# Transposes in 64-row halves, gathered in large groups, and inverse rows moved to other PSUM tiles, in a fused convolution and gated-MLP training step

## The chip, the cores and the metric

The kernel runs on one core of a Trainium2 chip, as one launch. The metric is the device time of that launch in microseconds. A core has a matrix engine (TensorE, here PE, with weight loads listed apart as PEld), a vector engine (VectorE, DVE), a scalar engine (ScalarE, ACT), GpSimd (POOL) and SyncE (SP). SP, ACT and POOL each have a queue from which they issue DMA transfers. SBUF is the working memory with 128 partitions; PSUM, in eight banks of 2 KB a partition, is where PE writes.

## What is computed

The reference is a forward pass and its gradient with respect to nine inputs:

```python
xn = layernorm(A_q)                                  # 2048 rows, 1024 columns
kv = shifted(A_k, A_shift_k) * A_v                   # four taps
y  = irfft(rfft(kv, 4096) * rfft(A_ssm_k, 4096))[:2048] + kv * A_ssm_D
s  = xn * y
h  = (xn @ w_gate) * (xn @ w_up)                     # 3584 columns
g  = silu(h @ w_down)
out = A_q + s * g
# then: gradients of all nine inputs for grad_out
```

All inputs and outputs are bfloat16. The long convolution runs down the rows, one for each of the 1024 columns.

## The kernel before

A Tile scheduler places the instructions of each engine; a few are pinned to their program order. PE does its work strictly in that order. The stages are:

*Layer norm and first gate blocks (to about 60 us).* `layer_norm` normalizes row blocks of 128. PE turns each 128x128 piece by a transpose (a matmul with the identity `ident`) into a PSUM tile `tr` of the pool `ps_st`, ACT copies it to `XNT`. The last eight blocks are put into `turn_rows` and turned later by `turn_late` (L617, L618), which `gu_unit` calls.

*The forward stage (60 to about 555 us).* `gu_unit` (L656 to L693) computes the gate and up products for four row blocks of one slab of 256 columns: for each block eight matmuls of 512 columns (1.7 us) into `psg`, an ACT copy to `gut`, then `flush(5)`, which calls what was put off five blocks earlier with `defer`. `multiply` makes the product `hN` on DVE, and stores it. `turn` transposes `hN` in eight 128x128 pieces (L689) into the one PSUM tile of the pool `ps_tr` (one bank), ACT copies them to `hT` (L691), and `store` writes `hT` to `HTd` on SP's queue. There are 14 slabs of 16 row blocks.

Between the blocks stands the convolution, `conv_forward`, a generator: `pump` runs it forward after each block as far as a planned share of its DVE work (`F_TOTAL`, less 0.95 times the PE work that `pe_us` counts). For each of eight column groups `ds` of 128 it does: `h_rows` (16 transposes of filter rows, L752 and L754, in two groups of eight through `ps_tr`, each with an ACT copy to `hx`); forward transforms of filter and data (`fwd4_half` or `fwd8_half`: PE matmuls into `psF` of the pool `ps_cv`, two tiles of two banks, ACT copies to `SP`, then sums on DVE); `product` and the inverse (`inv_dft` or `inv8`) on DVE into `HX`; and one column group later `tail`: the inverse rows, matmuls of `HX` with the table `TI` (`inv8_rows` L446, `inv_rows` L457) into `psY` of the pool `ps_y` (one bank), two rows at a time in four steps, each with an ACT copy to `yf` (L773). The table `TI` is made by `turn_tables` (L193) in four groups, also through `psY`. During the forward stage PSUM is full: `ps_y` 1, `ps_tr` 1, `ps_gu` 2, `ps_cv` 4 banks.

*Down projection and gates (about 508 to 710 us).* `bm_mm` (L994) multiplies `HTd`'s rows with `w_down`, 28 pairs of 512-column matmuls a row block, into `psbm`. The last column group's four tail steps stand behind pairs 52, 55, 58 and 61 of the late row blocks, by the tuple `at`. `gate` does each row block on DVE: `so`, `gg`, `dbm`, `dy` and others.

*The rest (710 to 1917 us)*: gradients, dense matmuls (L1441, L1458, L1541, L1603) with the backward convolution beside them.

`st` and `cld` issue on POOL's queue (L66), `ld` on SP's (L61), `sta` on ACT's (L72); `tt` is a DVE operation (L213), `stt` another (L284).

Of the kernel before, what the change touches and what calls it, by code (L numbers as in the profile page):

```python
# [19 lines left out]
def build_kernel(  # L20
# [11 lines left out]
    nc = tc.nc  # L32
# [153 lines left out]
    def turn_tables(psp):  # L186

        for j in range(2):
            for rq in range(2):
                ps = psp.tile([P, 4, 2, P], BF16, name="psY")  # L190
                for i in range(4):
                    for k in range(2):
                        nc.tensor.transpose(ps[:, i, k, :], T4[j][:, 4 * rq + i, k, :], ident[:])  # L193
                nc.scalar.copy(out=TI[:, j, 4 * rq:4 * rq + 4], in_=ps[:])
                yield

# [251 lines left out]

    def inv_rows(G, psp, rp):

        ps = psp.tile([P, 2, 256], F32, name="psY")
        for i in range(2):
            r = 2 * rp + i
            n = 0
            for j in range(2):
                for k in range(2):
                    nc.tensor.matmul(ps[:, i, :], TI[:, j, r, k, :], gseg(G, r, j, k),  # L457
                                     start=(n == 0), stop=(n == 3))
                    n += 1
        return ps  # L460

# [60 lines left out]
    fg = pool("fg", 2, side="right")  # L522
    ps_y = pool("ps_y", 1, space=PSUM)
    ps_tr = pool("ps_tr", 1, space=PSUM)
    ps_gu = pool("ps_gu", 2, space=PSUM)
    ps_st = pool("ps_st", 4, space=PSUM)

    busy = ps_st.tile([P, 4, P], F32, name="tr")

# [33 lines left out]
    turn_rows = []  # L563

    def layer_norm(b0, n, x4):
        def small(name, dt=F32):
# [21 lines left out]
        for i in range(n):  # L588
            b = b0 + i
            q, qi = divmod(b, 4)  # L590
            last = V.tensor_scalar(x4[:, i, :], x4[:, i, :], mv[:, i, 0:1], RSTD[:, b:b + 1], op0=SUB, op1=MUL)
            if b < 2:
                for hh in range(2):
                    ps = ps_st.tile([P, 4, P], BF16, name="tr")
                    for dc in range(4):
                        d0 = (4 * hh + dc) * P
                        tr_ln[0] = nc.tensor.transpose(ps[:, dc, :], x4[:, i, d0:d0 + P], ident[:])
                    act_copy[0] = nc.scalar.copy(out=XNT[0][:, 4 * hh:4 * hh + 4, b * P:b * P + P], in_=ps[:])
                if b == 0:
                    with tc.issue_after(tr_ln[0].ins):  # L600
                        keep_busy(10)
                continue
            if b0 >= 8:
                turn_rows.append((x4[:, i, :], q, qi))
                continue
            ps = ps_st.tile([P, DC, P], BF16, name="tr")
            for dc in range(DC):
                tr_ln[0] = nc.tensor.transpose(ps[:, dc, :], x4[:, i, dc * P:(dc + 1) * P], ident[:])
            act_copy[0] = nc.scalar.copy(out=XNT[q][:, :, qi * P:(qi + 1) * P], in_=ps[:])
        c, r0 = divmod(b0, 8)  # L610
        return last, root, st(xnn[:, c, r0:r0 + n, :], x4[:, 0:n, :])

    def turn_late():
        for i, (x, q, qi) in enumerate(turn_rows):
            ps = ps_st.tile([P, DC, P], BF16, name="tr")
            for dc in range(DC):
                tr_ln[0] = nc.tensor.transpose(ps[:, dc, :], x[:, dc * P:(dc + 1) * P], ident[:])  # L617
            act_copy[0] = nc.scalar.copy(out=XNT[q][:, :, qi * P:(qi + 1) * P], in_=ps[:])  # L618
        turn_rows.clear()
# [3 lines left out]
    later = []  # L623
    gu_mm = [None]

    def defer(fn):
# [10 lines left out]
    hn = [nop]  # L637
    chunk = [0]

    def gu_unit(sl, b0, n, w, tick):  # L640
# [26 lines left out]
        def multiply():  # L667
            with tc.issue_after(last.ins) if b0 + n <= 4 and chunk[0] <= 2 else nullcontext():
                by_half = lambda t: t.rearrange("p i (a f) -> p a i f", a=2)
                tt(hN[:, :, 0:n], by_half(gut[:, 0, 0:n]), by_half(gut[:, 1, 0:n]), MUL)  # L670
            st(Hd[sl][:, :, b0:b0 + n, :], hN[:, :, 0:n])
            defer(turn)
        hn[0] = multiply

        def store(hT):
# [3 lines left out]
            if n == 4:  # L679
                ht_st[0] = ld(to[q0:q0 + 2].rearrange("q f a s -> f q (a s)"), hT[:].rearrange("f q a i s -> f q (a i s)"))  # L680
            else:
                ht_st[0] = ld(to[q0, :, :, i0 * P:(i0 + n) * P], hT[:, 0, :, 0:n].rearrange("f a i s -> f a (i s)"))

        def turn():
            hT = fg.tile([P, 2, 2, 2, P], BF16, name="hT") if chunk[0] > 5 else lnp.tile([P, 2, 2, 2, P], BF16, name="hT_s", bufs=5)
            ps = ps_tr.tile([P, 2, 2, 2, P], BF16, name="tr")
            for a in range(2):
                for i in range(n):
                    nc.tensor.transpose(ps[:, i // 2, a, i % 2, :], hN[:, a, i, :], ident[:])  # L689
            if n == 4:  # L690
                nc.scalar.copy(out=hT[:], in_=ps[:])  # L691
            else:
                nc.scalar.copy(out=hT[:, 0, :, 0:n], in_=ps[:, 0, :, 0:n])  # L693
            store(hT)

    h_out = []
    ht_st = [None]
    EIGHT = ((0, 0), (0, 1), (5, 0), (6, 0), (7, 0), (7, 1))
# [7 lines left out]
    def conv_forward():  # L706
# [35 lines left out]

        def h_rows(ds, c):
            if ds == 8:
                return
            hrow = S_["h", ds]
            if c == 0:
                S_["hx"] = cf.tile([P, NB, P], BF16, name="hx")
            pe_us[0] += 0.47
            ps = ps_tr.tile([P, 8, P], BF16, name="tr")  # L750
            with tc.issue_after(tr_ln[0].ins):
                nc.tensor.transpose(ps[:, 0, :], hrow[:, c, :, 0], ident[:])  # L752
            for r in range(1, 8):
                nc.tensor.transpose(ps[:, r, :], hrow[:, c, :, r], ident[:])  # L754
            nc.scalar.activation(S_["hx"][:, 8 * c:8 * c + 8, :], ps[:], ACT.Copy, scale=WSC)
            if c == 1:
                h_out.append(ds)
                if ds + 1 < 8:
                    load_h(ds + 1)

# [3 lines left out]
        def tail(ds):  # L764
# [3 lines left out]
            else:  # L768
                yf = krow[:].rearrange("p a b d -> p (a b d)")[:, 0:NB * P].rearrange("p (b d) -> p b d", b=NB)
            for rp in range(4):  # L770
                ps = (inv8_rows if ds in INV8 else inv_rows)(G, ps_y, rp)
                pe_us[0] += 0.45 if ds in INV8 else 0.9
                nc.scalar.copy(out=by_res(yf, rp), in_=rowps(ps))  # L773
                if ds == 7 and rp < 2:
                    nc.scalar.copy(out=y_first[0][:, 2 * rp:2 * rp + 2, 7 * P:8 * P], in_=yf[:, 2 * rp:2 * rp + 2])
                if rp == 3:
                    st(YFd[:, :, ds * P:(ds + 1) * P], yf)
# [48 lines left out]
        yield 3.9  # L826
        h_rows(0, 0)
        h_rows(0, 1)
        yield 0.1
        tl = turn_tables(ps_y)  # L830
        sp = [half(0, S_["hx"], i, Dz[:, 0:P]) for i in range(2)]
        for ds in range(8):
# [13 lines left out]
            else:  # L846
                yield from transform(ds, 0, sp, KX, own_room(HX), lambda i: sph.append(half(ds, S_["hx"], i, D0)), nop)
                S_["kst"] = st(KFd[ds], KX[:])
            next(tl, None)
            room = cf.tile([P, 4, 256], F32, name="room", tag="hx")[:] if eight else None  # L850
            yield from transform(ds, int(ds > 0), sph, HX if ds else KX, room, nop1 if eight else lambda c: h_rows(ds + 1, c),
                                 lambda: next(tl, None))
            if ds == 0:
                S_["kst"] = st(KFd[0], KX[:])
            if eight:
                h_rows(ds + 1, 0)
            turned(HX, 1, 0, 1)
            yield 1.3
            if eight:
                h_rows(ds + 1, 1)  # L860
            if ds == 7:
# [22 lines left out]

    F_TOTAL = 4 * SHIFT_W + 3.0 + 8 * (0.5 + FWD4_W + 1.3 + PROD_W + INV_W) + 10.0 - 0.95 * 8 * (4 * 1.75 + 0.95 + 4 * 0.9)
    F_TOTAL += len(EIGHT) * (FWD8_W - 9.6 + 0.95 * 1.75) - 2.0
# [119 lines left out]
    assert not conv_state["forward"]  # L1006
    ps_cv.release()
    ps_bm = pool("ps_bm", 2, side="right", space=PSUM)
    pss = [ps_bm.tile([P, D], F32, name="psbm") for i in range(2)]
# [245 lines left out]
    def gate(b, ps, parts=None):  # L1255
# [23 lines left out]
        def turn():  # L1279
            ps = ps_tr.tile([P, DC, P], BF16, name=tr_name[0])  # L1280
            for dc in range(DC):
                nc.tensor.transpose(ps[:, dc, :], dbm[:, dc * P:(dc + 1) * P], ident[:])
            nc.scalar.copy(out=DBMT[b // 4][:, :, (b % 4) * P:(b % 4 + 1) * P], in_=ps[:])
        if b >= 12:
# [51 lines left out]

    at = (52, 55, 58, 61)
    for n in range(at[3] + 1):
        mm = late_mm(n)
# [25 lines left out]
    rows_in[4] = gate_rows(4, 0, 2) + gate_rows(4, 2, 3, [y_4])  # L1365
    done = at[3] + 1
    while done < 2 * NF:
# [6 lines left out]
    for bp in range(2, 8):  # L1374
# [18 lines left out]
        for i in range(2):  # L1393
# [7 lines left out]
            gate(2 * bp + i, ps_of[2 * bp + i])  # L1401
    for p_ in (ps_bx, ps_tr, ps_y, ps_bm, mi, mo, mt, mh[1], mh[0]):
        p_.release()
# [363 lines left out]
```

## Time and profile before

| what | us |
| --- | --- |
| runs | 1917.67, 1919.29, 1920.26 (median 1919.29) |
| span of the profiled execution, from first to last instruction | 1916.6 |
| PE busy in that span | 1905.7 |
| DVE busy | 1557.1 |
| ACT busy | 640.0 |
| transposes of h (L689), 432 + 16 records | 33.1 + 1.9 |
| transposes of filter rows (L752, L754), 128 records | 3.5 + 9.6 |
| late normalized rows (L617), 64 records | 3.9 |
| inverse rows (L446 and L457 from `HX`), 176 records | 12.0 + 12.8 |

The page gives no time of the profiled execution but its span. The busy times of matmuls are of records that overlap: each ends later than the next one starts, so a group's busy time counts the end of its last one too. The timeline, by starts, tells what a group takes of PE.

### The profile page before, as it was taken

The numbers are of one execution on the slowest core, as the hardware profiler recorded it, in microseconds if no ns is written. First come the engines' busy times: TensorE is split into PE (matmuls) and PEld (weight loads), VectorE is DVE, ScalarE is ACT, GpSimd is POOL, SyncE is SP. The second block draws the span as 40 slices with busy tenths as digits, with TensorE's granted clock in tenths as the row PEclk, the third lists the DMA queues.
The fourth block names the chain that finished last, engine by engine and source line by source line (L and its number), as shares of the span: only waits on it lengthen the run. The fifth ranks groups of instructions, "written<-read, shape, count | busy, mean of one in ns | idle before, by whom it ended". The sixth has DMA issues, their size and how long they took to land. (4 is left out here: it accounts for less than half of the span.)

```text
span 1916.6 us, 27330 instructions
## 1 busy us (share of the span) xinstructions
PE 1905.7 (99%) x10915; PEld 1024.9 (53%) x10915; DVE 1557.1 (81%) x1723; ACT 640.0 (33%) x946; POOL 334.5 (17%) x465
## 2 busy tenths in 40 slices
PE   8999999999999999999999999999999999999999
PEld 5555555545544456666666665664444444444444
DVE  8999999999997556887999999999995205788862
ACT  5864555646433233432222222222222102011121
POOL 5121212111113220001031221111212101111120
PEclk9999999999999999999999999999999999999999
DMA  8776867668679997677887698585787999999962
GB/s 293 271 261 216 265 209 234 211 234 299 237 246 287 316 287 250 205 240 236 269 271 261 220 263 270 180 286 177 217 255 173 206 205 191 184 184 195 193 180 97
DMA packets 425487, 444.28 MB, mean 232 GB/s; under 512 B 268784, under 2 KB 343180, under 8 KB 410896
## 3 DMA queue, kind: packets, MB, share of 16 engines
q1 hardware_dynamic: 367888, 239.03, 46.9%
q0 software_dynamic: 41152, 174.15, 29.1%
q10 hardware_dynamic: 16320, 29.36, 4.1%
q8 instruction: 85, 1.39, 0.3%
q14 instruction: 42, 0.34, 0.1%
HBM read 193.87 MB, written 189.84 MB: 200 GB/s over the span
## 5 line engine op out<-in xcount | busy, mean ns | idle before, releaser
L656 PE MATMUL psg<-wslab,U 128*128 128x512 bf16 x1792 | 407.3, 379 | 3.0 <-DMA wslab<-in_B_w_gate_dram 2.0
L1458 PE MATMUL psb<-U,U 128*128 128x512 bf16 x1792 | 397.1, 379 | 0.0
L1603 PE MATMUL psx<-U,dgut 128*128 128x512 bf16 x1536 | 333.0, 379 | 0.5 <-DVE dxn L213 0.5
L1603 PEld LDWEIGHTS <-dgut 128*128 128x128 bf16 x1792 | 175.3, 98 | 212.1 <-issue 0.8
L1458 PEld LDWEIGHTS <-U 128*128 128x128 bf16 x1792 | 175.2, 98 | 198.0
L656 PEld LDWEIGHTS <-U 128*128 128x128 bf16 x1792 | 172.2, 98 | 187.4 <-issue 2.5
L1441 PE MATMUL psb<-wdt,U 128*128 128x256 bf16 x1792 | 205.6, 273 | 0.0
L213 DVE TENSOR_TENSOR W<-W 128x1024 f32<-128x1024 f32 (+1 forms) x192 | 189.1, 1001 | 4.2
L1441 PEld LDWEIGHTS <-U 128*128 128x128 bf16 x1792 | 175.3, 98 | 29.2
L1541 PE MATMUL psb<-U,U 128*128 128x512 bf16 x816 | 177.3, 379 | 0.0
L1463 ACT CAST wb<-psb 128x512 bf16<-128x512 f32 x112 | 65.6, 586 | 315.4 <-PE psb L1458 310.5
L1208 DVE SCALAR_TENSOR_TENSOR dkp<-dkT,kT 128x1024 bf16<-128x1024 bf16 (+2 forms) x64 | 78.3, 1224 | 104.0 <-DMA dkT<-DKSHd 102.2
L994 PE MATMUL psbm<-U,ht 128*128 128x512 bf16 x672 | 146.0, 379 | 0.0
L1541 PEld LDWEIGHTS <-U 128*128 128x128 bf16 x896 | 87.4, 98 | 104.3
L658 ACT CAST gut<-psg 128x512 bf16<-128x512 f32 x156 | 91.3, 588 | 120.0 <-PE psg L656 119.1
L1635 ACT ACTIVATE dx_t<-dxn 128x1024 bf16<-128x1024 f32 x15 | 15.9, 1057 | 324.2 <-DVE dxn L213 320.3
L994 PEld LDWEIGHTS <-ht 128*128 128x128 bf16 x672 | 65.6, 98 | 78.0
L213 DVE TENSOR_TENSOR U<-U,dht 128x2048 bf16<-128x2048 bf16 x56 | 68.3, 1221 | 46.4 <-ACT dht L1443 46.4
L1443 ACT CAST dht<-psb 128x512 bf16<-128x512 f32 x112 | 65.6, 587 | 116.3 <-PE psb L1441 116.3
L66 POOL DMA_DIRECT2D Hd<-hN x54 | 37.1, 686 | 292.3 <-DVE hN L213 289.4
L1582 ACT CAST wbs<-psb 128x512 bf16<-128x512 f32 x51 | 29.9, 586 | 145.4 <-PE psb L1541 137.3
L213 DVE TENSOR_TENSOR W<-SP 128x1024 f32<-128x1024 f32 x64 | 74.5, 1219 | 2.5 <-ACT SP L296 1.7
(261 smaller groups left out, 2386.3 us busy)
## 6 DMA issues: line engine op xcount, KB each, us to landing
U<-GUd SPq DMA_DIRECT2D x28, 1024.0 KB, 8.7
DGd<-U SPq DMA_DIRECT2D x28, 1024.0 KB, 6.5
GUd<-gut ACTq DMA_DIRECT2D x39, 512.0 KB, 5.5
out_dram<-wb SPq DMA_DIRECT2D x112, 128.0 KB, 4.8
U<-Hd SPq DMA_DIRECT2D x14, 1024.0 KB, 5.9
Hd<-hN POOLq DMA_DIRECT2D x54, 256.0 KB, 4.2
HTd<-hT SPq DMA_DIRECT2D x52, 256.0 KB, 3.9
ht<-HTd SPq DMA_DIRECT2D x18, 512.0 KB, 7.7
```

What stands on the lines that cost most here:

```text
L66: ins = nc.gpsimd.dma_start(out=out, in_=in_)
L213: pinned(V.tensor_tensor(o, a, b, op))
L656: gu_mm[0] = nc.tensor.matmul(ps[:], XNT[q][:, dc, qi * P:(qi + 1) * P], w[:, dc].rearrange("p a f -> p (a f)"), start=(dc == 0), stop=(dc ...
L658: nc.scalar.copy(out=gut[:, :, i], in_=ps[:].rearrange("p (a f) -> p a f", a=2))
L994: mm = nc.tensor.matmul(ps[:, dh * 512:(dh + 1) * 512], ht(fc)[:, i * P:(i + 1) * P], WD[fc // 4][:, fc % 4, dh * 512:(dh + 1) * 512], sta ...
L1208: ins = V.scalar_tensor_tensor(prod[:].rearrange("p r d -> p (r d)")[:, lo:H], dkT[:, 0, lo:H], 1.0, kT[:, 0, 13 + m + lo:13 + m + H], op0 ...
L1441: nc.tensor.matmul(ps[:, x * SLW:(x + 1) * SLW], DBMT[2 * hf + g][:, dc, (b % 4) * P:(b % 4 + 1) * P], wdt[:, dc, :], start=(dc == 0), sto ...
L1443: nc.scalar.copy(out=dht[:, 2 * e:2 * e + 2].rearrange("p b f -> p (b f)"), in_=ps[:])
L1458: nc.tensor.matmul(ps[:], XN[b // 4][:, b % 4, dc * P:(dc + 1) * P], dgus[b // 8][:, :, b % 8], start=(b == 0), stop=(b == NB - 1))
L1463: nc.scalar.copy(out=wb[:, dc % 2].rearrange("p a f -> p (a f)"), in_=ps[:])
L1541: nc.tensor.matmul(ps, h[:, f, b, :], DBM[b // 4][:, b % 4, dh * 512:(dh + 1) * 512], start=(b == 0), stop=(b == NB - 1))
L1603: nc.tensor.matmul(ps[:, dh * 512:(dh + 1) * 512], t[n][:, f, i * P:(i + 1) * P], WGU[n][:, f, dh * 512:(dh + 1) * 512], start=(n == 0 and ...
```

## The change

- `turn_halves` transposes a 128-row piece as two matmuls: rows 0 to 63 with the upper left quarter of the identity, rows 64 to 127 with the lower right one. Each has 64 columns and writes 64 of the 128 output columns, the two into different PSUM banks.
- h of slabs 2 to 13: `turn_pair` turns two units (eight row blocks, 32 halves) in one group, into a `ps_tr` tile of two banks; two ACT copies put the halves together in `hT` (one buffer, twice as large), and one store of 512 KB follows. Slabs 0 and 1 keep `turn`.
- Filter rows: one group of 32 halves for each column group, with two ACT copies behind it.
- Late normalized rows: `turn_late` turns four row blocks in one group of 64 halves, with the four copies behind it. The layer norm's tiles become parts of one tile `turns` of four banks.
- Inverse rows: four rows at a time in two steps (`inv_quad`) into tiles of two banks, `psF` of `ps_cv`, and after `ps_cv` is released `ps_tr`'s. `turn_tables` makes two groups of 16 transposes in `psF` tiles. The pool `ps_y` is gone, and its bank goes to `ps_tr`.
- The last column group's two steps stand behind pairs 62 and 69. The planner's prices follow.

```diff
     def turn_tables(psp):
         for j in range(2):
-            for rq in range(2):
-                ps = psp.tile([P, 4, 2, P], BF16, name="psY")
...
+            ps = psp.tile([P, 8, 2, P], BF16, name="psT", tag="psF")
...
-    def inv_rows(G, psp, rp):
...
+    def inv_quad(G, ps, rq, eight):
+        for i in range(4):
+            r = 4 * rq + i
             n = 0
-            for j in range(2):
+            for j in range(1 if eight else 2):
                 for k in range(2):
+                    inv_mm[0] = nc.tensor.matmul(ps[:, i, :], TI[:, j, r, k, :], G[:, 2 * r + k, :] if eight else gseg(G, r, j, k),
+                                                 start=(n == 0), stop=(n == (1 if eight else 3)))
                     n += 1
...
-    ps_y = pool("ps_y", 1, space=PSUM)
-    ps_st = pool("ps_st", 4, space=PSUM)
+    ps_st = pool("ps_st", 1, space=PSUM)
+    turns = ps_st.tile([P, 4, 2, 4, P], BF16, name="tr")
...
+    def turn_halves(ps, src):
+        for hh in range(2):
+            rows = slice(64 * hh, 64 * hh + 64)
+            ins = nc.tensor.transpose(ps(hh), src[rows], ident[rows, rows])
+        return ins
+
+    def halves(x):
+        return x.rearrange("p b (h u) -> p h b u", h=2)
...
     def turn_late():
+        ps = turns[:].rearrange("p (h j) i b x -> p h j i (b x)", h=2).rearrange("p h j i (a u) -> p h (j i) a u", u=64)
         for i, (x, q, qi) in enumerate(turn_rows):
-            ps = ps_st.tile([P, DC, P], BF16, name="tr")
             for dc in range(DC):
-                tr_ln[0] = nc.tensor.transpose(ps[:, dc, :], x[:, dc * P:(dc + 1) * P], ident[:])
-            act_copy[0] = nc.scalar.copy(out=XNT[q][:, :, qi * P:(qi + 1) * P], in_=ps[:])
+                tr_ln[0] = turn_halves(lambda hh: ps[:, hh, i, dc], x[:, dc * P:(dc + 1) * P])
+        for i, (x, q, qi) in enumerate(turn_rows):
+            act_copy[0] = nc.scalar.copy(out=halves(XNT[q][:, :, qi * P:(qi + 1) * P]), in_=ps[:, :, i])
...
+    def tr_tile():
+        return ps_tr.tile([P, 2, 8, P], BF16, name="tr")
...
-            defer(turn)
+            if sl < 2:
+                defer(turn)
+            else:
+                mate.append(hN)
+                if b0 % 8 == 4:
+                    defer(turn_pair)
...
+        def turn_pair():
+            hT = fg.tile([P, 4, 2, 2, P], BF16, name="hT", bufs=1)
+            two_, mate[:] = mate[0:2], mate[2:]
+            ps = tr_tile()[:].rearrange("p h b x -> p h (b x)").rearrange("p h (b u) -> p h b u", u=64)
+            for qq in range(4):
+                for a in range(2):
+                    for i in range(2):
+                        turn_halves(lambda hh: ps[:, hh, 4 * qq + 2 * a + i], two_[qq // 2][:, a, qq % 2 * 2 + i, :])
+            to = HTd[b0 // 8][sl // 4][:, :, 2 * (sl % 4):2 * (sl % 4) + 2, :]
+            for g in range(2):
+                nc.scalar.copy(out=halves(hT[:, 2 * g:2 * g + 2].rearrange("p q a i s -> p (q a i) s")), in_=ps[:, :, 8 * g:8 * g + 8])
+            ht_st[0] = ld(to.rearrange("q f a s -> f q (a s)"), hT[:].rearrange("f q a i s -> f q (a i s)"))
...
-        def h_rows(ds, c):
+        def h_rows(ds):
...
-            pe_us[0] += 0.47
-            ps = ps_tr.tile([P, 8, P], BF16, name="tr")
+            pe_us[0] += 0.67
+            ps = tr_tile()[:].rearrange("p h b x -> p h (b x)").rearrange("p h (b u) -> p h b u", u=64)
             with tc.issue_after(tr_ln[0].ins):
-                nc.tensor.transpose(ps[:, 0, :], hrow[:, c, :, 0], ident[:])
-            for r in range(1, 8):
-                nc.tensor.transpose(ps[:, r, :], hrow[:, c, :, r], ident[:])
-            nc.scalar.activation(S_["hx"][:, 8 * c:8 * c + 8, :], ps[:], ACT.Copy, scale=WSC)
+                turn_halves(lambda hh: ps[:, hh, 0], hrow[:, 0, :, 0])
+            for b in range(1, 16):
+                turn_halves(lambda hh: ps[:, hh, b], hrow[:, b // 8, :, b % 8])
+            for c in range(2):
+                nc.scalar.activation(halves(hx[:, 8 * c:8 * c + 8, :]), ps[:, :, 8 * c:8 * c + 8], ACT.Copy, scale=WSC)
...
-            for rp in range(4):
-                ps = (inv8_rows if ds in INV8 else inv_rows)(G, ps_y, rp)
-                pe_us[0] += 0.45 if ds in INV8 else 0.9
+            for rq in range(2):
+                ps = (ps_tr if cv_gone else ps_cv).tile([P, 4, 256], F32, name="psI", tag="tr" if cv_gone else "psF")
+                inv_quad(G, ps, rq, ds in INV8)
+                pe_us[0] += 0.9 if ds in INV8 else 1.8
...
-    at = (52, 55, 58, 61)
-    for n in range(at[3] + 1):
+    at = (62, 69)
+    for n in range(at[1] + 1):
```

## The prediction

> **What bounds the kernel now.** I read the page's busy shares and its 40 slices first, then a table by stage, then the timeline of the forward stage for prices, then the timeline at the end of that stage.
>
> ```profile
> PE 1905.7 (99%) x10915; PEld 1024.9 (53%) x10915; DVE 1557.1 (81%) x1723; ACT 640.0 (33%) x946; POOL 334.5 (17%) x465
> PE   8999999999999999999999999999999999999999
> DVE  8999999999997556887999999999995205788862
> ```
>
> TensorE (PE) is busy throughout, and its waits on others add up to 6.5 us: every microsecond of PE work that goes away shortens the kernel, unless another engine takes over. The candidate is VectorE (DVE), at 9 tenths in slices 1 to 11. By stage (columns: stretch, length, busy time with count of PE, weight loads, DVE, ACT, POOL, clock, DMA share, GB/s):
>
> ```profile
> 80.00:555.00 475.00, 474.34 (x2867) 258.13 (x2866) 470.36 (x453) 254.63 (x357) 75.18 (x106) 1.00 0.71 241
> 555.00:620.00 65.00, 65.00 (x311) 30.23 (x309) 50.70 (x83) 20.37 (x23) 21.36 (x33) 1.00 0.94 262
> 620.00:740.00 120.00, 119.94 (x685) 65.37 (x683) 56.83 (x84) 38.09 (x45) 21.41 (x34) 1.00 1.06 314
> ```
>
> From 80 to 555 us DVE is 99% busy beside a full PE. All transposes that the change touches lie before 514 us. So PE can run ahead of DVE there only as far as the next thing that it needs from DVE. The prices of PE work (start, length, idle before in brackets):
>
> ```profile
> 402.46 0.61 PE L689 MATMUL tr<-ident,hN 128*128 128x128 bf16 x8
> 402.91 7.07 PE L656 MATMUL psg<-wslab,U 128*128 128x512 bf16 x32
> 409.82 0.61 PE L689 MATMUL tr<-ident,hN 128*128 128x128 bf16 x8
> 421.07 1.04 PE L235 MATMUL psF<-kv,TF 128*128 128x256 bf16 x8
> 421.94 3.62 PE L656 MATMUL psg<-wslab,U 128*128 128x512 bf16 x16
> ```
>
> Start to start, eight transposes take 0.45 us (56 ns each, 128 columns), eight 256-column matmuls 0.87 (109 ns), 32 of 512 columns 6.91 (216 ns): 0.417 ns a column and 2.5 ns beside it. By this slope 64 columns are 29 ns, an estimate. A record lasts longer than its slot: 0.61 - 7 x 0.056 = 0.219 us for a transpose, 163 ns beyond its 56; I call that the tail. The filter rows are dearer:
>
> ```profile
> L689 PEld LDWEIGHTS <-hN 128*128 128x128 bf16 x432 | 28.7, 98 | 12.1 <-issue 0.3
> L754 PEld LDWEIGHTS <-U 128*128 128x128 bf16 x112 | 8.2, 147 | 3.0 <-issue 2.8
> 453.95 1.02 ACT L691 COPY hT<-tr 128x1024 bf16<-128x1024 bf16 x1
> 454.15 0.81 PE L656 MATMUL psg<-wslab,U 128*128 128x512 bf16 x3
> 455.02 0.22 PE L752 MATMUL tr<-ident,U 128*128 128x128 bf16 x1
> 455.07 0.60 PE L754 MATMUL tr<-ident,U 128*128 128x128 bf16 x7
> 455.51 1.24 PE L656 MATMUL psg<-wslab,U 128*128 128x512 bf16 x5
> ```
>
> Their weights are read with a stride of eight elements: a load lasts 147 ns instead of 98, and eight of them take 0.49 us (61 ns each). The group is also late: due at 454.15 + 3 x 0.216 = 454.80, it starts at 455.02, when the copy of the h group before it has freed the one `ps_tr` tile (454.97). Summed in this way, the 16 groups lose 2.1 us.
>
> ```profile
> 552.59 2.49 DVE L284 SCALAR_TENSOR_TENSOR HX<-W 128x512 bf16<-128x512 f32 x4
> 556.61 0.60 PE L446 MATMUL psY<-HX,TI 128*128 128x256 bf16 x4
> 561.82 0.60 PE L446 MATMUL psY<-HX,TI 128*128 128x256 bf16 x4
> 562.51 0.69 DVE L213 TENSOR_TENSOR so<-U,U 128x1024 bf16<-128x1024 bf16 x1 [3.81 <-issue]
> ```
>
> Here PE meets DVE for the last time in the stage: the last inverse rows need `HX`, finished at 555.1, and PE asks for them at 556.6. The slack is 1.5 us.
>
> **The change, part by part.** *Transposes.* 384 of h (slabs 2 to 13), 128 of filter rows and 64 late normalized rows, 576 in all, become 1152 halves of 64 columns. I count in units of 16 old transposes: 24 of h, 4 late, 8 of filter rows, in 34 unbroken runs. An old h or late unit costs 16 x 0.056 = 0.90 us. A new one has 16 pairs. If the two halves of a pair run side by side a pair is 29 ns and the unit 0.47; if one after the other, 58 ns and 0.93. No row shows it; I take side by side, since the halves use separate rows of the array and write separate banks. Going into and out of the other shape is in no row either: between nothing and the tail, 0.16 us each way. I take 0.1 each way, so 0.67 a unit: 28 x (0.90 - 0.67) = 6.4 us gained.
>
> The Trainium skill (TensorE: Matmul & The Clock Gate, Part 3, The mechanism) says that matmuls of different row groups start about 4 ns apart; by it a pair would be 33 ns, an estimate, and the gain 28 x 16 x 0.004 = 1.8 us less. No run so far shows this.
>
> *Filter rows.* Old unit: 2 x 0.49 = 0.98. New: 32 strided loads. If the loads of a pair lie side by side, 61 ns a pair, 0.98; one after the other 1.95; if half the rows load in half the time, 0.47. I take the middle one, whose 61 ns a row shows: 0.98 + 0.2 = 1.18, a loss of 8 x 0.2 = 1.6 us. The 2.1 us of late starts go, since the two groups are one. New ones come: in the built order three runs start 1.95 us of PE work after another run ended, while the two copies of that one need 0.2 + 2 x 1.02 us and sometimes a 0.59 us gate copy between: some 0.5 us each, -1.5. Net -1.0.
>
> *Inverse rows and tables.* The same matmuls in fewer, longer groups: nothing on PE. Two ACT copies of 0.59 become one of 1.02; ACT is 54% busy in the stage (254.6 of 475). The shared tiles (`psF`, two of them) are free in time: in the built order 1.7 us of gate matmuls or more lie between a forward half and an inverse group, against 1.02 us for a copy.
>
> *Copies and stores of h.* 1024 elements a copy as before, hidden under PE; a second `hT` buffer isn't needed, as pairs are some 14 us apart. The SP queue issues 24 stores of 512 KB for 48 of 256 KB. A slab load behind them has a slab's time of slack (issued at 437.7, needed after 455). One down-weight load now stands before the last slab load and waits for DVE's last use of U7; that ended at 417.6, 20 us before the slab load could issue. On POOL the store of y goes behind that of HX; y is read from 528 us on. The first `hN` of a pair is held for about ten blocks of 1.8 us; three buffers give twelve.
>
> *The last inverse groups* move from pair 52 to 62 of the down-projection matmuls, and from 61 to 69. Ten pairs are 20 x 0.216 = 4.3 us of PE work. So PE can gain 1.5 + 4.3 = 5.8 us before it waits for DVE at this place. DVE itself can be some 0.9 us earlier, as its first shift waited for the late transposes (two groups, 2 x 2 x 0.23). The ceiling of the gain is thus 6.7 us: anything beyond becomes a wait for `HX`. DVE's gates started when the last inverse group ended (562.4, next line 562.51); relative to PE they come 8 pairs, 3.5 us, later. Cover: from 598 us DVE waits for PE's rows again (50.7 of 65 us busy, then 56.8 of 120), and a row's PSUM tile is used again three rows (36 us) later. Behind this, nothing is changed.
>
> **The sum.** 6.4 - 1.0 = 5.4 us, under the ceiling of 6.7. Profiled span 1916.6 - 5.4 = 1911.2; the runs' median of 1919.29 lies 2.7 us above the span, which I keep: 1913.9. The terms' far ends: all side by side and free, 28 x 0.43 + 8 x 0.51 + 2.1 = 18.2, cut to 6.7 (1912.6); nothing side by side, with full tails and loads one after the other, 28 x (0.90 - 1.26) + 8 x (0.98 - 2.28) + 0.6 = -19.9 (1939).
>
> **Rivals.**
> *Slower: the halves take turns.* One mechanism, in every run: a pair costs 58 ns, a unit with 0.2 for its ends 1.13. h and late rows lose 28 x 0.23 = 6.4, filter rows 8 x 0.15 = 1.2, late starts give 0.6 back: +7.0, 1926.3; with the strided loads one after the other, too, a filter unit is 2.15, 8 x 1.17 = 9.4 instead of 1.2, 1934.5. It decides from some 42 ns a pair on, where a unit costs its old 0.88. For it: twice the loads and matmuls, and PE already takes one transpose in exactly its 128 columns, with the load hidden. Against: nothing shows separate rows held back by each other. PE being full, all of the loss would show.
>
> *No change: the ends eat the gain.* Each run pays the whole tail twice, 0.33 us: a unit is 0.79, 28 x 0.11 = 3.1; filter rows 8 x -0.33 = -2.6; late starts +0.6; gain 1.1, 1918.2. For it: 34 runs have 68 ends, and every matmul's record shows the 163 ns. Against: a tail hides wherever the next one needs nothing of it.
> The Trainium skill (TensorEngine Tiling (Array Packing), Tiling Modes, Key Properties) speaks for this rival: changing the tiling mode drains the TensorE. No run so far shows it.
>
> *The ceiling holds the gain.* If runs are cheaper than I think, PE waits for `HX` at the first moved group, and the time is 1912.6 to 1913.5. It is on the forecast's side.
>
> That the program doesn't do what it says is out: the built order has 1152 transposes of 64 columns in 34 runs.
>
> **How the numbers follow.** Forecast with its ceiling 0.55 (own range 1911 to 1916.5), no change 0.18, slower 0.27. About 0.2% (3.8 us) can be told from no change. A tenth of the forecast's case falls short of it, and some of the slower case too: faster 0.53, same 0.20, slower 0.27. The range goes from 1910.5 (the ceiling less a run's spread) up to 1928, which leaves out the worse half of the slower case.
>
> **What would show it.** A run of 32 halves of h should last about 0.6 to 0.7 us from the matmul before to the one after, 0.47 inside; 0.9 and more says that they take turns. A gap at its two ends above 0.1 us speaks for the second rival. Filter runs near 1.2 us: loads side by side. A wait of PE for `HX` at the first moved inverse group says that the ceiling was met. The prediction is wrong if PE waits for ACT before many runs, or if DVE stops being full between 80 and 550.

## The result, and the profile after

| | us |
|---|---|
| before, median of 20 executions in the same comparison | 1917.91 (1917.47 to 1922.92) |
| after, median of 20 | 1922.07 (1920.5 to 1925.32) |
| ratio after to before | 1.0019, 95% interval 1.0013 to 1.0025 |
| profiled execution after: span | 1919.9 (before: 1916.6) |

The change made the kernel slower, by 3.6 us by the ratio and 4.2 by the medians; the forecast was 5.4 us faster. Its twenty times fall into two groups: ten with a mean granted clock of 0.998 or more (median 1921.2) and ten with 0.997 (median 1923.2). The profiled execution is of the first. A step of this size belongs to an early spell of half clock that the profiles of e3, e7 and e8 show (see there); of the changed kernel no profile has it. The page of the changed kernel, its busy times and two rows of the 40 slices:

```profile
PE 1893.1 (99%) x11351; PEld 1011.8 (53%) x11491; DVE 1557.3 (81%) x1723; ACT 637.0 (33%) x927; POOL 332.5 (17%) x465
...
PE   8999999999899999999999999999999999999999
...
DVE  8999999999978555887899999999996205788862
```

PE has 12.6 us less busy time than before (1893.1 against 1905.7; some 140 matmul records are missing, by the count of the weight loads) and yet the span is longer. There is one new dent: an 8 in slice 11, at 480 to 528 us. In the table by stage (columns as in the prediction), 80 to 555 us shows 9.3 us less PE beside a DVE that is as full as it was:

```profile
80.00:555.00 475.00, 465.07 (x3299) 246.43 (x3356) 470.39 (x454) 253.55 (x342) 74.72 (x106) 0.99 0.73 241
503.80:507.70 3.90, 3.90 (x33) 1.76 (x31) 3.79 (x7) 0.58 (x1) 0.68 (x1) 1.00 0.89 240
507.70:510.10 2.40, 0.05 (x4) 0.00 (x0) 2.40 (x4) 0.00 (x0) 0.00 (x0) 1.00 0.98 339
510.10:513.20 3.10, 0.00 (x0) 0.00 (x0) 3.00 (x5) 0.00 (x0) 0.55 (x1) 0.51 1.05 420
513.20:517.00 3.80, 3.55 (x23) 1.65 (x25) 3.77 (x4) 1.93 (x2) 0.67 (x1) 0.50 0.45 167
517.00:520.00 3.00, 3.00 (x19) 1.76 (x18) 3.00 (x5) 1.01 (x1) 0.00 (x0) 1.00 0.45 152
```

The finer rows below the first hold the loss of this execution. From 507.75 to 513.2 us PE does nothing. In the third of them the clock column falls from 1.00 to 0.51, and it stays at 0.50 until PE has worked for 3.8 us. The timeline of PE there (start, length, what, idle before in brackets):

```profile
500.33 3.63 PE L673 MATMUL psg<-wslab,U 128*128 128x512 bf16 x15
503.80 3.62 PE L1032 MATMUL psbm<-U,U 128*128 128x512 bf16 x16
507.35 0.41 PE L571 MATMUL tr<-ident,hN 64*128 64x64 bf16 x16
513.23 0.61 PE L571 MATMUL tr<-ident,hN 64*128 64x64 bf16 x16 [5.47 <-DVE hN L212]
513.77 0.61 PE L1032 MATMUL psbm<-U,U 128*128 128x512 bf16 x1
514.60 2.87 PE L1032 MATMUL psbm<-U,U 128*128 128x512 bf16 x7 [0.22 <-issue]
517.30 1.04 PE L455 MATMUL psI<-HX,TI 128*128 128x256 bf16 x8
```

The second half of the last `turn_pair` waits 5.5 us for the last `hN`. Behind it, the weight loads of the 512-column matmuls start every 0.427 us from 513.77 to 516.73, where at full clock it is every 0.216; from 513.23 to the inverse group at 517.30 these 16 halves and nine matmuls take 4.07 us, where 0.33 (the halves in e3 below) and 9 x 0.216 make 2.27 us at full clock. So the half clock costs about 1.8 us. The same stretch of the kernel before, whose lines the prediction did not show:

```profile
503.22 3.62 PE L656 MATMUL psg<-wslab,U 128*128 128x512 bf16 x16
506.67 0.60 PE L446 MATMUL psY<-HX,TI 128*128 128x256 bf16 x4
507.11 1.03 PE L994 MATMUL psbm<-U,U 128*128 128x512 bf16 x4
508.00 0.60 PE L446 MATMUL psY<-HX,TI 128*128 128x256 bf16 x4
508.43 2.75 PE L994 MATMUL psbm<-U,U 128*128 128x512 bf16 x12
511.02 0.60 PE L446 MATMUL psY<-HX,TI 128*128 128x256 bf16 x4
511.45 0.61 PE L689 MATMUL tr<-ident,hN 128*128 128x128 bf16 x8
511.90 1.24 PE L994 MATMUL psbm<-U,U 128*128 128x512 bf16 x5
513.21 0.61 PE L689 MATMUL tr<-ident,hN 128*128 128x128 bf16 x8
```

Here 21 down projection matmuls and 12 inverse matmuls stand between the last gate matmul and the last transposes, 21 x 0.216 + 12 x 0.109 = 5.8 us; after the change it is 16 matmuls, 3.5 us. So PE comes to the last `hN` earlier for two reasons: it is 2.9 us ahead when its gate matmuls end (503.80, before at 506.67), and 2.4 us of work that stood in front now stand behind: the 12 inverse matmuls (1.3 us) and five down projection matmuls (1.1 us). The shorter transposes of this last run add 0.2. And the `hN` itself, first line after, second before, comes no sooner:

```profile
512.48 0.69 DVE L212 TENSOR_TENSOR hN<-gut 128x1024 bf16<-128x1024 bf16 x1
```

```profile
511.76 0.68 DVE L213 TENSOR_TENSOR hN<-gut 128x1024 bf16<-128x1024 bf16 x1
```

PE asked for it 0.8 us after it landed before the change, and 5.4 us before it landed after it. The terms add up: 0.8 of slack, less 2.9, 2.4 and 0.2, less the 0.7 us by which the `hN` is later, is 5.4 us short. The lead of 2.9 us, 3.1 with this last run, becomes a lag of 4.1 us by 527 us, through 5.5 of waiting and about 1.8 of half clock. Of this 0.7 comes back in the last dx stage, whose cause was not sought, and 3.3 remain in the span. The weight loads of the halves (busy, mean ns, idle before) end the table; there are 1152, as built:

```profile
L571 PEld LDWEIGHTS <-hN 64*128 64x128 bf16 x768 | 12.8, 95 | 15.6 <-DVE hN L212 6.0 <-issue 5.9 <-DVE HX L212 1.7
L571 PEld LDWEIGHTS <-U 64*128 64x128 bf16 x384 | 10.7, 141 | 4.4 <-issue 3.3 <-DVE U L603 1.2
```

### The profile page after: what moved, and what is told of

The parts are those of the page before. It is cut to its first block, busy times and chain, and to the rows that moved or that the text cites. A ratio compares the mean times of both kernels' runs of the same rounds, so it can differ in the third digit from the quotient of the medians.

```text
span 1919.9 us, 28250 instructions
## 1 busy us (share of the span) xinstructions
PE 1893.1 (99%) x11351; PEld 1011.8 (53%) x11491; DVE 1557.3 (81%) x1723; ACT 637.0 (33%) x927; POOL 332.5 (17%) x465
## 4 chain that ended last, share of the span: by engine, by line
PE 84%; DVE 12%; issue 2%; ACT 1%; DMA 1%; SPq 0%; ACTq 0%; DVEq 0%
PE psb L1497 20%; PE psx L1642 20%; PE psb L1480 10%; PE psbm L1032 10%; PE psb L1580 9%; PE psg L673 8%; DVE W L212 4%; DVE HX L212 2%; PE psF L234 2%; DVE KX L212 1%; DVE U L212 1%; DVE m L212 1%; DVE hN L212 1%; PE psY L1191 1%; PE psY L445 1%
## 5 line engine op out<-in xcount | busy, mean ns | idle before, releaser
L673 PE MATMUL psg<-wslab,U 128*128 128x512 bf16 x1728 | 398.1, 379 | 6.5 <-DMA wslab<-in_B_w_gate_dram 1.6
```

Source lines behind the costliest of these rows:

```text
L673: gu_mm[0] = nc.tensor.matmul(ps[:], XNT[q][:, dc, qi * P:(qi + 1) * P], w[:, dc].rearrange("p a f -> p (a f)"), start=(dc == 0), stop=(dc ...
```

## The experiments

All are edits of the changed kernel, in two comparisons on two chips; medians of the kernel before were 1917.54 us in the first (e1 to e4) and 1917.64 in the second (e5 to e8). Intervals are of the ratio to the kernel before.

### e1: the last h transposes later

```diff
-    with tc.issue_after(bm_first(range(4)).ins):
+    with tc.issue_after(bm_first(range(12)).ins):
         flush()
...
-    fc_ = 4
+    fc_ = 12
```

> One part of the changed kernel moved: the last 32 h transposes go behind 48 instead of 16 of the down projection's first matmuls, so TensorE reaches them some 7 us later. Theory 1 (TensorE runs into the last hN of VectorE: 5.9 us of idle time at 507 to 513 us, then about 4 us at half the clock, some 1.9 us more): hN lands at about 512.5 to 513 us as before the move, TensorE asks for it after that, no idle time over 0.5 us there, granted clock 1.00 in the windows around it, the lead of 3.3 us that the first down projection matmul has is kept, and the time is about 1914.5 us (1913 to 1916.5). Theory 2 (the loss lies elsewhere: the early phase, the transfers, or the halves themselves): about the changed kernel's 1922 us.

Measured: 1914.12 us, ratio 0.9981 (0.9972 to 0.9990). One shift in the order, by two numbers that belong together, makes the change faster than the kernel before. The windows of e1 at this place (the granted clock stands behind the counts of POOL) and its timeline:

```profile
507.00:514.00 7.00, 7.00 (x38) 3.58 (x37) 6.86 (x10) 1.01 (x1) 1.23 (x2) 1.00 0.95 353
514.00:520.00 6.00, 6.00 (x63) 3.23 (x61) 5.97 (x9) 1.99 (x3) 0.00 (x0) 1.00 0.40 134
```

```profile
503.50 5.34 PE L1032 MATMUL psbm<-U,U 128*128 128x512 bf16 x24
508.68 1.04 PE L455 MATMUL psI<-HX,TI 128*128 128x256 bf16 x8
509.55 5.34 PE L1032 MATMUL psbm<-U,U 128*128 128x512 bf16 x24
514.83 0.64 PE L571 MATMUL tr<-ident,hN 64*128 64x64 bf16 x32
515.40 3.63 PE L1032 MATMUL psbm<-U,U 128*128 128x512 bf16 x16
```

PE is full through both windows, the clock is 1.00, and the 32 halves find both `hN` there (the last starts on DVE at 512.19). The eleven times fall into two groups: six at 1913.4 to 1914.1 with a mean clock of 1.000, five at 1914.9 to 1916.0 with 0.999. That second group is the early loss, below.

### e2: full transposes in the new groups

```diff
-            ps = tr_tile()[:].rearrange("p h b x -> p h (b x)").rearrange("p h (b u) -> p h b u", u=64)
+            ps = tr_tile()[:].rearrange("p h b x -> p (h b) x")
...
-                        turn_halves(lambda hh: ps[:, hh, 4 * qq + 2 * a + i], two_[qq // 2][:, a, qq % 2 * 2 + i, :])
+                        nc.tensor.transpose(ps[:, 4 * qq + 2 * a + i, :], two_[qq // 2][:, a, qq % 2 * 2 + i, :], ident[:])
...
```

> One part undone: h, the filter rows and the late normalized rows are turned by 128-column transposes again, in the changed kernel's groups and order; everything else as changed. TensorE's work up to the last h transposes grows by some 4.7 us (28 runs of h at 0.23 us more, filter rows less 1.6 us). Theory 1 (the gain is lost in front of the last hN and in the clock behind it): TensorE comes to the last h transposes about 5 us later, waits 1 us or less, and its clock stays at 1.00: 1919 to 1921 us, not slower than the changed kernel. Theory 2 (what the halves save does reach the end, and the loss is another part's): slower than the changed kernel by about 4.7 us, 1926 to 1927 us.

Measured: 1924.72 us (1921.26 to 1925.87), ratio 1.0032 (1.0020 to 1.0045): the median lies between the two theories. The five executions spread over 4.6 us and the interval overlaps that of the changed kernel, so how much slower e2 is than that isn't shown. The profiled execution is the fastest of the five. In it theory 1's numbers for the wait are wrong. PE's wait:

```profile
PE tr L704 <- DVE hN L212: 3.1, 1, 3.1
```

It is 3.1 us, not 1 or less, and the clock fell to half again. When its gate matmuls end (505.91 us) PE leads before by only 0.8 us. I had reckoned with the lead alone and overlooked the order: the 2.4 us of work that the new groups let fall behind the last transposes. With almost no lead the order alone already brings a wait. The halves in the old order were not run.

### e3: matmuls in the idle time

```diff
+    mm = bm_first(range(4))
+    dm = ps_gu.tile([P, 512], F32, name="psg")
+    with tc.issue_after(mm.ins):
+        for n in range(20):
+            mm = nc.tensor.matmul(dm[:], ident[:], Wbc[:, 0, 0:512], start=True, stop=True)
+    with tc.issue_after(mm.ins):
         flush()
```

> 20 matmuls of 512 columns that nothing reads (4.3 us of extra work, no output changed) stand between the 16 down projection matmuls and the last h transposes of the changed kernel, where TensorE was idle. Theory 1a (the clock drop after the idle time costs some 1.9 us by itself): idle time left about 1.5 us, the matmuls behind it start every 0.216 us from the first on instead of every 0.427 us, and the kernel is faster than the changed one by 1.5 to 2 us (about 1920.2 us) with 4.3 us more of matmuls. Theory 1b (idle time alone, the clock takes no part): the same as the changed kernel, 1922 us within 0.4. Theory 2 (no slack there, TensorE is bound through this place): slower by up to 4.3 us.

Measured: 1919.60 us, ratio 1.0012 (1.0004 to 1.0021): faster than the changed kernel by 2.5 us by the medians and 1.3 by the ratios, with 4.3 us more of matmuls in it. In its timeline the wait is short and the nine matmuls behind it start every 0.216 us, 2.12 us in all:

```profile
508.61 4.48 PE L1053 MATMUL psg<-Wbc,ident 128*128 128x512 bf16 x20
513.02 0.41 PE L571 MATMUL tr<-ident,hN 64*128 64x64 bf16 x16
514.60 0.41 PE L571 MATMUL tr<-ident,hN 64*128 64x64 bf16 x16 [1.16 <-DVE hN L212]
514.93 2.12 PE L1032 MATMUL psbm<-U,U 128*128 128x512 bf16 x9
```

Theory 1b (no part for the clock) and theory 2 fall: the half clock has a price of its own. The plain medians mix executions with and without the early half clock (with it are ten of 20 of the changed kernel and three of 11 of e3). Without it the medians are 1921.2 and 1919.5, a difference of 1.7 us, near the 1.8 of the trace.

### e4: the layer norm's PSUM as before

```diff
-    ps_st = pool("ps_st", 1, space=PSUM)
-    turns = ps_st.tile([P, 4, 2, 4, P], BF16, name="tr")
+    ps_st = pool("ps_st", 4, space=PSUM)
...
-                tr_ln[0] = turn_halves(lambda hh: ps[:, hh, i, dc], x[:, dc * P:(dc + 1) * P])
+                tr_ln[0] = nc.tensor.transpose(ps[:, dc, :], x[:, dc * P:(dc + 1) * P], ident[:])
...
```

> One part undone: the PSUM of the layer norm is the four single tiles of the kernel before, with its four groups of 128-column transposes for the late rows; h and the filter rows stay as changed. The early order of VectorE and TensorE is then that of before. Theory 1 (VectorE's timetable begins 1.45 us later in the changed kernel, since three statistics of a late chunk stand ahead of a normalization, and the last hN comes later by it): VectorE's first shift starts at about 51.0 instead of 52.45 us, the last hN lands about 1 us earlier (511.8 instead of 512.5), the wait and the half clock behind it stay: about 1921 us, 1 to 1.5 us faster than the changed kernel. Theory 2 (the early 1.2 to 2.4 us are TensorE's own and are hidden by the later wait): 1922 us within 0.4, the wait as much longer as TensorE is earlier.

Measured: 1920.47 us, ratio 1.0013 (1.0005 to 1.0022): faster than the changed kernel by 1.6 us by the medians and 1.2 by the ratios, with intervals that overlap. The first shift of DVE starts at 51.80 us, not at 51.0: there it waits for the load of `k`. Still the last `hN` starts at 510.67 us (1.8 us earlier than 512.48, more than expected, and why so much was not sought), and PE's wait for it is 5.3 us, about what it was. The early place, DVE in the changed kernel and then in the kernel before:

```profile
18.47 1.88 DVE L584 BATCH_NORM_STATS2 bst<-U 128x6 f32<-128x512 bf16 x3 [1.92 <-DMA U<-in_A_q_dram]
20.27 1.10 DVE L212 TENSOR_TENSOR hN_s<-gut_s 128x256 bf16<-128x256 bf16 x1
...
26.30 1.92 DVE L603 TENSOR_SCALAR U<-U,mv,RSTD 128x1024 bf16<-128x1024 bf16 x4
```

```profile
17.25 1.10 DVE L213 TENSOR_TENSOR hN_s<-gut_s 128x256 bf16<-128x256 bf16 x1 [0.56 <-ACT gut_s L658]
...
25.07 1.92 DVE L591 TENSOR_SCALAR U<-U,mv,RSTD 128x1024 bf16<-128x1024 bf16 x4
```

With one tile for all of the layer norm's turns, the scheduler puts an `hN_s` (1.10 us) behind three statistics that wait for a load. Before, it ran in front of them, at 17.25, in DVE's idle time. It is the tile and not the halves that does this: e2 keeps the tile, has no halves, and shows the new order; e4 has the old one. The normalization then starts at 26.30 instead of 25.07 us, and 0.7 us of PE work that stood in front of it now stands behind. PE waits for it 2.9 us at 24 to 27 us instead of 0.95.

### e5: e1 and e4 together; e6: filter rows by full transposes too

e6 is e5 with this part of e2's edit:

```diff
-                turn_halves(lambda hh: ps[:, hh, b], hrow[:, b // 8, :, b % 8])
+                nc.tensor.transpose(ps[:, b, :], hrow[:, b // 8, :, b % 8], ident[:])
```

> The two edits of e1 (last h transposes behind 48 down projection matmuls) and e4 (layer norm's PSUM and its late transposes as before) together. Theory 1 (the loss is the last hN's wait with its half clock, and beside it the early order with its own idle time of 2.6 to 2.9 us at 24 to 27 us, after which the clock halves in some executions): both are away, so the executions no longer fall into two groups, granted clock 1.00 in all, and the time is that of e1's better group less the 1.3 us that e4's first down projection matmul is ahead of e1's: 1912.5 us (1911.5 to 1913.5). Rival (VectorE's timetable holds: a further lead of TensorE is only waited out, at the last hN or the last inverse rows): 1914 us, with a new wait for VectorE of a us or more between 500 and 560 us.

> e5 with the filter rows turned by 16 transposes of 128 columns in their one group, h still by halves. By rows a group costs 0.99 us in e2 and 1.20 in e1, so 8 x 0.21 = 1.7 us of TensorE's work goes. Theory 1 (TensorE sets the end from there on): 1.0 to 1.7 us faster than e5, about 1911 us. Rival (that far ahead TensorE waits for VectorE's kv and HX in the forward and inverse transforms): the same as e5 within 0.5 us, with idle time at the transforms grown by what was saved.

Measured: e5 1913.27 us (1911.92 to 1913.91), ratio 0.9975 (0.9966 to 0.9984); e6 1913.06 (1912.25 to 1914.84), ratio 0.9977 (0.9968 to 0.9987). Every execution of both has a mean clock of 1.000: the two groups are gone. e5 is 4.4 us faster than the kernel before. It lies 0.9 us below e1's median, less than the 1.6 expected there, and the two intervals overlap. In e6 the rival is right: its eight filter units take 1.5 us less of PE (8.1 against 9.6 us), and the time is the same. The waits of PE from 45 us on, e5 first, then e6 (total, times, longest):

```profile
PE psF L234 <- DVE kv L212: 0.7, 1, 0.7
PE psg L666 <- ACT gut L668: 0.4, 1, 0.4
PE psF L234 <- ACT SP L256: 0.2, 1, 0.2
```

```profile
PE psg L666 <- ACT gut L668: 1.7, 1, 1.7
PE psF L234 <- DVE kv L212: 1.4, 1, 1.4
PE psF L234 <- ACT SP L256: 0.5, 2, 0.2
```

They grow from 1.3 to 3.6 us. Here the forward stage is held by the engines that feed it.

### e7: full transposes, last ones late; e8: the last ones half as late

e7 is e1 and e2; e8 is e1 with `range(8)` and `fc_ = 8`.

> e1 and e2 together: 128-column transposes everywhere, in the changed kernel's groups, with the last h transposes behind 48 down projection matmuls. It measures what the 64-row tiles are worth once nothing stands in their way. Theory 1: e2's first gate matmuls at 500 us are 2.5 us behind e1's, though its runs of transposes cost 4.7 us more, because e1 waits some 1.8 us more for kv and SP in the forward transforms; so 1914.1 + 2.5 = 1916.6 us, with clock 1.00 and no wait at the last hN. Rival (the halves' whole 4.7 us arrives): 1918.8 us. Rival (halves worth nothing, all is the grouping): 1914 us.

> As e1 with the last h transposes behind 32 instead of 48 down projection matmuls (16 in the changed kernel): the idle time is cut by 16 matmuls of 0.216 us and 8 inverse matmuls of 0.11 us, from 5.5 to 1.2 us. Theory 1 (the wait costs its length, and the half clock comes only behind a long one, as e3's 1.2 us of idle time had none): idle time of 1 to 1.5 us at the last hN, clock 1.00 there, about 1.2 us slower than e1, 1915.3 us. Rival (any wait there brings the half clock): 1917 us or more, with matmul starts every 0.43 us behind the wait.

Measured: e7 1918.16 us (1916.25 to 1920.06), ratio 1.0001 (0.9992 to 1.0010); e8 1916.55 (1914.60 to 1917.26), ratio 0.9991 (0.9982 to 1.0000). Both medians are above theory 1, nearer to a rival, and the reason is the early place. Here are e8's wait there, from its timeline, and the clock in its windows:

```profile
26.97 0.62 PE L620 MATMUL tr<-ident,U 128*128 128x128 bf16 x8 [3.23 <-DVE U L603]
```

```profile
27.00:28.00 1.00, 1.00 (x11) 0.76 (x12) 1.00 (x3) 0.37 (x1) 0.00 (x0) 0.93 0.73 258
28.00:29.00 1.00, 1.00 (x6) 0.45 (x4) 1.00 (x4) 1.00 (x2) 0.42 (x1) 0.50 0.02 4
29.00:30.00 1.00, 1.00 (x9) 0.72 (x8) 1.00 (x3) 0.41 (x2) 1.00 (x3) 0.50 0.32 131
```

The clock is at half, although PE is full. The profiles of e3 and e7 show it too (0.50 at 28 to 29 us, behind waits of 2.85 and 2.53 us); those of the changed kernel and of e1 do not, behind 2.86 and 2.62 us. So it comes in some executions only. A spell of 3.4 us at half clock lowers the mean of an execution by 0.001, which is the step between the groups of executions. Taking those with a mean clock of 1.000, a choice made after the result, the medians are 1913.9 for e1 (6 of 11), 1915.3 for e8 (4 of 11) and 1917.1 for e7 (6 of 11). By these e8 is theory 1's number, 1.3 us above e1 for 1.1 us of waiting, and its clock at 507 to 520 us is 1.00. e7 is 3.1 us above e1: that is what the 64-row tiles are worth here, filter rows included, nearer to theory 1's 2.5 than to 4.7.

## Why the prediction was wrong

**The step that failed is the ceiling**: "So PE can gain 1.5 + 4.3 = 5.8 us before it waits for DVE at this place", with 0.9 us added for an earlier DVE. I rested it on the sentence that PE meets DVE there "for the last time in the stage", and asked only about that last meeting. The prediction's own sentence, that PE can run ahead "only as far as the next thing that it needs from DVE", was the right test; I didn't put it to the things in between. The first place where a gain runs out decides, and it is the last `hN`, 42 us earlier: its slack before the change was 0.8 us, less the 2.4 us of work that the new order takes from in front of it, so below nothing. At the place that I named, DVE is done at 555.8 us and PE comes at 565.02:

```profile
553.32 2.50 DVE L283 SCALAR_TENSOR_TENSOR HX<-W 128x512 bf16<-128x512 f32 x4
565.02 1.04 PE L455 MATMUL psI<-HX,TI 128*128 128x256 bf16 x8
```

It was not a limit without the stall either: in e1 `HX` is done at 555.5 and PE comes at 557.29. e1, which changes only the order, came out at 1914.12 with the rest of the change as it is, beside the forecast of 1913.9. That they are so close is luck. The forecast started from 1919.29, the median of three executions; the larger samples gave 1917.5 to 1917.9. From its own before, e1 gains 3.4 to 3.6 us, not 5.4.

**Where the rest of the 5.4 went.** By the rows of the traces some 6.3 us of PE work before 503 us is gone in e1 (h 23 x 0.224, late rows 0.8, filter rows 0.4), and PE is 3.2 us ahead there. Longer waits took most of the difference: 1.7 us more at 24 us, 0.6 more for an ACT copy at 41 us, 1.1 for `kv` and `SP` (forward transforms). The sum had no term for waits of PE for DVE in front of the ceiling.

**The stall's second price** stood in no step: behind the 5.5 us of idle time the clock halves, about another 1.8 us (e3). Where I wrote "anything beyond becomes a wait", a wait was priced at its own length.

**The halves: right.** A run of 32 halves of h costs 0.669 us from the matmul before to the one after (forecast 0.67): 0.451 inside, 29 ns a pair, and 0.10 and 0.09 at its ends. e1's lines show it: from 509.55 to 515.40 are 5.85 us, 24 x 0.216 and the run. Within a pair the second half starts 3 to 4 ns after the first, and the next pair 26 ns later; so the estimate of 33 ns a pair was too high. That they take turns (the slower rival) and that the ends eat the gain (the no-change rival) are both refuted; the kernel became slower by a third way. The Trainium skill (TensorEngine Tiling (Array Packing), Tiling Modes, Key Properties) says that a change of mode drains TensorE; the two ends agree, and measure 0.19 us together. Between 45 and 503 us the 32 runs cost 26.2 us in e1 and 30.9 in e2, summed from the starts of their neighbours in the trace; of these 4.7 us 3.1 reach the end (e7 against e1). e1 waits there for `kv` (0.7 us) and `SP` (0.4), e7 for neither; the small rest was not traced.

**Filter rows: the unit right, the net not.** A new unit measures 1.20 us (forecast 1.18). An old one with its late starts costs 2 x 0.63 = 1.25, and a full one in the new group 0.99 (e2), so the halves lose 0.2 us there, as forecast. The old late starts go, and the new close pairs for which I took off 1.5 us hardly show (e1's groups lie between 1.19 and 1.23). The net is +0.4, not -1.0 us.

**Inverse rows, "nothing on PE":** their matmuls do start every 0.109 us as before. But as work they were cover for the last `hN`, and 12 of them moved behind it, 1.3 of the 2.4 us. The edit that I costed at nothing took away cover, and I did not ask whose.

**DVE 0.9 us earlier: the wrong sign.** Its first shift starts at 52.45 us instead of 51.00; in e5, with the old order around `hN_s`, at 50.93. Undoing that part gave 1.2 to 1.6 us (e4 against the changed kernel) and 0.9 (e5 against e1); part of both is the half clock behind the longer wait at 24 us, and without the executions that have it 0.7 to 0.8 remain.

Of the signs that I named, "PE waits for ACT before many runs" did not come, and DVE stayed full. Neither was a sign of what happened.

## What to carry to other kernels

When PE work is taken out of a stage whose other engine is full, list every thing that PE asks of that engine, with the slack of each in the old trace, in order of time: the first small slack caps the gain, and work that the new order moves behind such a place must be taken off its slack. Price a new stall of PE of several us with the half clock behind it, and if it can't be avoided, move independent matmuls in front of it. Look for a change of order by the scheduler even where only buffers were changed.

## What the runs showed of the hardware

- Two 64-row transposes on separate rows run side by side: the second starts 3 to 4 ns after the first, and a pair takes 29 ns, where one 128-column transpose takes 56 ns (e1). With weights read at a stride of eight elements a pair takes 61 ns, about what a full transpose of such rows takes.
- The clock fell to half 2.2 to 4.1 us after PE had gone idle, and came back 2.9 to 4.4 us after PE had resumed. The half clock lasted 3.41 us in e2, e3, e7 and e8 and twice that, 6.83, in the changed kernel and e4. In e8 it fell 4.1 us after the wait had begun, 0.9 us after PE had resumed. In the profiles, waits of 1.2 us and the early 1.9 and 1.8 us of e2 and e4 did not bring it, 2.5 to 2.9 us did in e3 and e7 and not in e1 and the changed kernel, and all four waits of 3.1 us or more did. The Trainium skill (TensorE: Matmul & The Clock Gate, Part 1: The HAM clock gate, What's actually happening) gives one idle window of about 3.4 us for it, and a window that runs freely, not from the start of the idle time. That it comes in some executions and not in others agrees; that 2.53 us was enough in e7 does not.
